# Eight PSUM banks dealt 3/3/2 in place of 2/4/2 among DFT pieces, first-layer and second-layer products

## The chip, the cores and the metric

The kernel runs on one core of one Trainium2 chip. The metric is device time in microseconds (us), the median of three runs; lower is better. Besides the runs, one execution was taken by the hardware profiler, and every view shown here comes from that one.

TensorE (PE) multiplies, ScalarE (ACT) and VectorE (DVE) work element by element, GpSimd (POOL) and SyncE (SP) mostly issue DMAs here. PSUM is the memory that matmuls write; it has eight banks, each 128 partitions by 512 fp32 values. Every PSUM tile of this kernel takes one bank.

## The reference

For each of 8 batches of 3008 tokens by 256 channels, a spectral filter along the tokens, and then a two-layer network with a periodic activation on all 24,064 tokens:

```python
X = np.fft.rfft(x, axis=1)
Y = X * (filt_r + 1j * filt_i)[None]
x = np.fft.irfft(Y, n=3008, axis=1).reshape(24064, 256)
h = x @ w_in                                  # 256 -> 2048
g = h + np.sin(alpha * h) ** 2 / (alpha + 1e-09)
out = g @ w_out                               # 2048 -> 256
```

## The kernel before, in words

**The network.** It is worked in 48 chunks of tokens, 12 for each pair of batches: 44 of 512 columns and 4 of 384 (those with `c0 == 2560`: chunks 5, 17, 29 and 41). For each chunk, `hidden(k, jb)` runs for jb = 0 to 15: two accumulating matmuls (L540, one for each half of the 256 channels) write a first-layer block of 128 features by 512 tokens into a PSUM tile `ph`; ACT takes its sine with a phase (L544, `cos_all<-ph`); DVE joins both into `v` (L545, `v<-cos_all,ph`). Because L545 reads `ph` a second time, the bank is free only when L545 has ended. `project(k, u)` makes the second layer: for each block of 128 tokens, 16 matmuls with 256 columns (L557, `po<-w,v`) in two halves of eight, then an ACT copy (L565) and DMAs to the output.

**The spectral filter.** A DFT of 3008 = 47 x 64 in two stages, forward and back, for each batch, as small pieces: `first` (tile `pa`, L181), `forward` (`pb`, L201, evicted by ACT at L204, then the two halves are swapped by DMA into `xs`), `product` and `cross` (DVE, L215, L221, L222), `inverse` (`pc`, L232) and `last` (`pd`, L254). Most evictions go through `evac` (L160 on ACT, L162 on DVE), two on ACT for each one on DVE. Batch 0 is worked ahead of the network with tiles of the same names (`pa` L399, `pb` L431, `pc` L453, `pd` L343); warming matmuls on idle data (L381) fill TensorE's early waits. `last` writes `y`, the network's input.

**The order.** The kernel is scheduled by hand; each engine runs its list in the order in which the program issues it. The main loop goes through 49 chunk places of eight half-steps j: two first-layer products of chunk k, then pieces that are due (`slot`), then that half-step's share of second-layer halves of chunk k-1, then pieces again. Which halves fall on half-step j is `range(n_half * j // 8, n_half * (j + 1) // 8)`, with n_half = 8 for a chunk of 512 columns and 6 for one of 384. Pieces have due times in half-steps (`put`); the last `pd` matmul starts at 729.9 us.

**The pools.** PSUM tiles come from three pools: `fps` for all spectral pieces (tag "f"), `hps` for first-layer products (`ph`), and, before the network starts, for some of batch 0's tiles (`pa` of two in three pieces, `pb`, one `pd`), for warming tiles and for alpha's spread; `ops` for `po` and a few early tiles. A tile's first matmul waits until the instructions that read the bank's earlier tile have ended. TensorE works strictly in order, so whatever stands behind a waiting matmul waits too.

Of the kernel before, what the change touches and what calls it, by code (L numbers as in the profile page):

```python
# [15 lines left out]
PSUM = bass.MemoryType.PSUM  # L16
# [46 lines left out]
def kernel(  # L63
# [28 lines left out]
    def pool(name, bufs, space=None):  # L92
        kw = {} if space is None else {"space": space}
        return ctx.enter_context(tc.tile_pool(name=name, bufs=bufs, **kw))
# [8 lines left out]
    opool = pool("op", 3)  # L103
    vpool = pool("vp", 2)
    dpool = pool("dram", 2, DRAM)
    fps = pool("fps", 2, PSUM)
    hps = pool("hps", 4, PSUM)
    ops = pool("ops", 2, PSUM)

    wf_t = cpool.tile([NR, NK], FP16)  # L110
# [46 lines left out]
    def evac(dst, src, on_act=None):  # L157
        flip[0] = (flip[0] + 1) % 3
        if flip[0] if on_act is None else on_act:
            marks["act"] = nc.scalar.copy(out=dst, in_=src)  # L160
        else:
            marks["dve"] = nc.vector.tensor_copy(out=dst, in_=src)  # L162
# [213 lines left out]
    def warm_pe(n):  # L376

        warmed.append(n)
        ps = hps.tile([128, 512], FP32, name=f"warm_{len(warmed)}", tag="h")
        for i in range(n):  # L380
            nc.tensor.matmul(out=ps, lhsT=idle[:, 0:128], rhs=idle[:, 0:512], start=True, stop=True)  # L381
# [7 lines left out]
    def cast_x0(h):  # L389

        cs = slice(4 * C * h, 4 * C * h + 4 * C)
        evac(x0[0].rearrange("p n c -> p (n c)")[:, cs], x32[0:NR, cs], False)
# [1 line left out]
    cast_x0(0)  # L394
    nc.vector.reciprocal(out=rec, in_=al)
    for i in range(16):
        own, tag = (fps, "f") if i % 3 == 2 else (hps, "h")
        ps = own.tile([128, 512], FP32, name=f"pa_0_{i}", tag=tag)
        nc.tensor.matmul(out=ps, lhsT=wf0_t[0:NR], rhs=x0[i // 4][:, 2 * (i % 4):2 * (i % 4) + 2, :],  # L399
                         start=True, stop=True)  # L400
        evac(t1_0[:, 2 * i:2 * i + 2], ps.rearrange("p (n k c) -> p n c k", n=2, k=2), i % 2)
        if i == 1:
            warm_pe(3)
            cast_x0(1)
        if i < 15 and i % 4 == 3:
            warm_pe((2, 2, 2, 1)[i // 4])
# [56 lines left out]
    for g in range(6):  # L463
        own, tag = (t2pool, "t2") if g < 3 else (gpool, "g")
# [225 lines left out]
```

## Time and profile before

| what | value |
|---|---|
| runs, median (lowest to highest) | 789.85 us (789.4 to 790.68) |
| profiled execution, span | 786.7 us |
| granted TensorE clock, mean | 1.000 |
| first matmul of the first product of the network (L540) | 36.8 us |
| L540, one matmul with 512 columns, median | 379 ns |
| L544 on 128x512, median | 597 ns |
| L545 on 128x512, median | 681 ns |
| evictions of pa: ACT / DVE, median | 582 / 679 ns |
| evictions of pc: ACT / DVE, median | 592 / 685 ns |
| evictions of pb (ACT), median | 586 ns |

The span is from the first to the last instruction of the profiled execution; the runs' times include what lies around it, 3.15 us at the median. A matmul's own duration is longer than its distance to the next one, since they are pipelined: two readings of TensorE's progress, the busy time and the distance of starts, have to be kept apart. In groups, the part behind the bar is busy time, the mean of one instruction, and the idle time of that engine just before such instructions with what ended it. In the timeline, a row is start, length from the first start to the last end, engine, line, operation, tiles and shapes, and how many instructions it merges.

Busy time by stretch, from the windows view (all engines in us):

| stretch, us | what runs | PE | DVE | ACT | clock |
|---|---|---|---|---|---|
| 0 to 37 | batch 0's filter, weights | 32.20 | 30.34 | 24.97 | 1.00 |
| 37 to 48 | chunk 0, no second layer yet | 10.28 | 9.69 | 10.51 | 1.00 |
| 48 to 73 | batch 0's last pieces, batch 1's first | 22.31 | 19.39 | 18.81 | 1.00 |
| 73 to 86 | batch 1, forward | 12.81 | 10.73 | 10.78 | 1.00 |
| 86 to 118 | batch 1, filter and inverse | 31.12 | 30.55 | 25.62 | 1.00 |
| 118 to 130 | | 11.97 | 9.71 | 9.78 | 1.00 |
| 130 to 787 | the regular part | 652.83 | 547.21 | 515.99 | 1.00 |

### The profile page before, as it was taken

How to read it: one execution, taken by the hardware profiler on the slowest of the kernel's cores; microseconds unless marked ns; L12 is line 12 of the kernel's file. 1: busy time of each engine (PE TensorE's matmuls, PEld its weight loads, DVE VectorE, ACT ScalarE, POOL GpSimd, SP SyncE). 2: the span in 40 equal slices, each digit the busy share in tenths (PEclk: the TensorE clock that was granted, in tenths of full speed). 3: DMA queues.
4: the chain of work that ended last, by engine and by line, in shares of the span. 5: the costliest groups of instructions: out<-in, count | busy, mean ns of one | idle time of the engine just before them, and what ended most of it. 6: DMA issues, size and time to landing. Idle time of an engine off the chain costs nothing.

```text
span 786.7 us, 16619 instructions
## 1 busy us (share of the span) xinstructions
PE 773.5 (98%) x5799; PEld 535.0 (68%) x5799; DVE 657.6 (84%) x1172; ACT 616.5 (78%) x1208; POOL 79.5 (10%) x125
## 2 busy tenths in 40 slices
PE   8998999999999999999999999999999999999998
PEld 4756766666667766777666766777666776766666
DVE  7887997899878997799977998799987999777773
ACT  5797878888878887888877888788887887777674
POOL 6442000200020000200020000200002000000000
PEclk9999999999999999999999999999999999999999
DMA  9965568665473646554575454845556243421111
GB/s 213 258 131 157 113 145 223 153 123 133 134 198 84 134 99 195 143 120 110 120 200 128 103 106 139 224 87 113 129 155 181 61 99 81 117 62 28 41 41 54
DMA packets 87692, 100.99 MB, mean 128 GB/s; under 512 B 14488, under 2 KB 75944, under 8 KB 87608
## 3 DMA queue, kind: packets, MB, share of 16 engines
q1 hardware_dynamic: 78032, 73.73, 34.5%
q0 software_dynamic: 9360, 26.15, 17.7%
q8 instruction: 45, 0.74, 0.4%
q14 instruction: 39, 0.32, 0.1%
q10 hardware_dynamic: 216, 0.05, 0.0%
HBM read 55.72 MB, written 46.66 MB: 130 GB/s over the span
## 4 chain that ended last, share of the span: by engine, by line
PE 89%; DVE 5%; ACT 2%; DMA 2%; issue 1%; SPq 1%; ACTq 0%; DVEq 0%
PE po L557 39%; PE ph L540 38%; PE pa L181 3%; PE pd L254 2%; DVE v L545 2%; PE pb L201 2%; PE pc L232 2%; DMA xs<-xf 1%; ACT cos_all L544 1%; DMA al<-in_moe_alpha_dram 1%; PE warm L381 1%; PE pc L453 0%; SPq L585 0%; ACT t_h L160 0%; DVE filt_t L162 0%
## 5 line engine op out<-in xcount | busy, mean ns | idle before, releaser
L545 DVE SCALAR_TENSOR_TENSOR v<-cos_all,ph 128x512 f16<-128x512 f32 (+1 forms) x768 | 483.0, 672 | 108.1 <-ACT cos_all L544 104.8
L544 ACT ACTIVATE cos_all<-ph 128x512 f32<-128x512 f32 (+1 forms) x768 | 411.1, 592 | 93.9 <-PE ph L540 92.9
L540 PE MATMUL ph<-y,w 128*128 128x512 f16 (+1 forms) x1536 | 388.4, 374 | 1.7 <-DVE y L162 0.9
L557 PE MATMUL po<-w,v 128*128 128x256 f16 x3008 | 389.5, 272 | 0.0
L557 PEld LDWEIGHTS <-v 128*128 128x128 f16 x3008 | 288.3, 98 | 77.7 <-issue 1.4
L540 PEld LDWEIGHTS <-w 128*128 128x128 f16 x1536 | 147.9, 98 | 106.5 <-issue 6.1
L565 ACT COPY o<-po 128x512 f32<-128x512 f32 (+1 forms) x97 | 55.6, 574 | 20.2 <-PE po L557 12.9
L204 ACT CAST xf<-pb 128x512 f16<-128x512 f32 x84 | 50.0, 595 | 16.4 <-PE pb L201 12.7
L193 POOL DMA_DIRECT2D t<-d x56 | 36.4, 669 | 204.6 <-DMA out_dram<-o 99.8
L160 ACT CAST t_h<-pa 96x512 f16<-96x512 f32 x74 | 43.3, 585 | 10.6 <-PE pa L181 10.5
L141 POOL DMA_DIRECT2D x<-in_x_dram x32 | 17.1, 536 | 298.2 <-PE pc L232 171.2
L160 ACT CAST y<-pd 128x376 f16<-128x376 f32 (+1 forms) x82 | 39.5, 482 | 8.8 <-PE pd L254 5.3
L254 PEld LDWEIGHTS <-t_a 96*128 96x128 f16 x448 | 31.3, 97 | 18.7 <-issue 0.4
L181 PE MATMUL pa<-x,wf_t 94*96 94x512 f16 x112 | 42.3, 381 | 1.6 <-ACT t_h L160 1.3
L160 ACT CAST g<-pc 128x512 f16<-128x512 f32 x58 | 34.4, 593 | 8.0 <-PE pc L232 7.7
L222 DVE TENSOR_TENSOR p<-p,xs 128x512 f16<-128x512 f16 x84 | 35.7, 425 | 2.9
L254 PE MATMUL pd<-wi_t,t_a 96*128 96x94 f16 x448 | 37.1, 204 | 0.0
L221 DVE TENSOR_TENSOR xs<-xs,filt_t 128x512 f16<-128x512 f16 x84 | 35.2, 420 | 0.8 <-DMA xs<-xf 0.8
L215 DVE TENSOR_TENSOR p<-xf,filt_t 128x512 f16<-128x512 f16 x84 | 35.2, 419 | 0.0
L232 PE MATMUL pc<-p,e_t 128*128 128x256 f16 x168 | 32.1, 273 | 0.8 <-ACT xf L204 0.5
L201 PE MATMUL pb<-t,d_t 128*128 128x256 f16 x168 | 32.1, 272 | 0.2
L162 DVE CAST y<-pd 128x376 f16<-128x376 f32 (+2 forms) x46 | 24.9, 544 | 1.5 <-PE pd L343 1.0
(66 smaller groups left out, 264.4 us busy)
## 6 DMA issues: line engine op xcount, KB each, us to landing
x<-in_x_dram POOLq DMA_DIRECT2D x30, 376.0 KB, 4.9
d<-t_h SPq DMA_DIRECT2D x28, 384.0 KB
t<-d POOLq DMA_DIRECT2D x56, 192.0 KB, 4.6
xs<-xf SPq DMA_DIRECT2D x168, 64.0 KB
d<-g SPq DMA_DIRECT2D x56, 192.0 KB
t_a<-d SPq DMA_DIRECT2D x28, 384.0 KB
out_dram<-o SPq DMA_DIRECT2D x104, 80.0 KB
w_out<-in_moe_w_out_dram SPq DMA_DIRECT2D x2, 1024.0 KB
```

Source lines behind the costliest of these rows:

```text
L160: marks["act"] = nc.scalar.copy(out=dst, in_=src)
L181: marks["pe"] = nc.tensor.matmul(out=ps[0:NK, :], lhsT=wf_t, rhs=self.x[ch][:, 2 * j:2 * j + 2, :], start=True, stop=True)
L193: nc.gpsimd.dma_start(out=self.t2[g][64 * p:64 * p + 64, :, :], in_=self.d1[a0:a0 + 6, :, :].rearrange("s n c -> n s c"))
L201: nc.tensor.matmul(out=ps[:, i, :], lhsT=d_t[:, s, :], rhs=self.t2[s // 6][:, s % 6, :], start=True, stop=True)
L204: nc.scalar.copy(out=self.xf[u], in_=ps)
L232: nc.tensor.matmul(out=ps[:, i, :], lhsT=e_t[:, 2 * w + i, :], rhs=pt[:, i, :], start=(k == 0), stop=(k == len(pr) - 1))
L254: nc.tensor.matmul(out=psv[:, i, :], rhs=wi_t, start=True, stop=True, lhsT=t4_h[ch // 2][0:NK, n0 % 16 + i, cb * 128:cb * 128 + 128])
L540: nc.tensor.matmul(out=ps[:, 0:n], lhsT=w1[:, cb, jb * 128:jb * 128 + 128], rhs=y_cols[:, cb, c0:c0 + n], start=(cb == 0), stop=(cb == 1))
L544: nc.scalar.activation(out=cs[:, 0:n], in_=ps[:, 0:n], func=AFT.Sin, bias=float(np.pi / 2))
L545: marks["snake"] = nc.vector.scalar_tensor_tensor(out=v[k][:, jb, 0:n], in0=cs[:, 0:n], scalar=-1.0, in1=ps[:, 0:n], op0=ALU.add, op1=ALU. ...
L557: nc.tensor.matmul(out=pso[k][:, t % 2, :], lhsT=v[k][:, jb, 128 * t:128 * t + 128], rhs=w2[:, jb, :], start=(jb == 0), stop=(jb == 15))
L565: nc.scalar.copy(out=o[:, i0:t % 2 + 1, :], in_=pso[k][:, i0:t % 2 + 1, :])
```

## The change

Two numbers of banks are exchanged, and the rule by which the 16 first-stage pieces of batch 0 take turns between the two pools changes with them: every second piece instead of every third goes to `fps`. `ops` keeps two. The sum stays at eight banks.

```diff
@@ -103,8 +103,8 @@
     dpool = pool("dram", 2, DRAM)
-    fps = pool("fps", 2, PSUM)
-    hps = pool("hps", 4, PSUM)
+    fps = pool("fps", 3, PSUM)
+    hps = pool("hps", 3, PSUM)
     ops = pool("ops", 2, PSUM)
@@ -394,7 +394,7 @@
     for i in range(16):
-        own, tag = (fps, "f") if i % 3 == 2 else (hps, "h")
+        own, tag = (fps, "f") if i % 2 else (hps, "h")
         ps = own.tile([128, 512], FP32, name=f"pa_0_{i}", tag=tag)
```

## The prediction

> **What bounds the kernel now.** I read the page first, for the busiest engine and the heaviest groups, then the durations of everything that touches a first-layer bank (ph), then the instructions in order of time at three places.
>
> ```profile
> span 786.7 us, 16619 instructions
> PE 773.5 (98%) x5799; PEld 535.0 (68%) x5799; DVE 657.6 (84%) x1172; ACT 616.5 (78%) x1208; POOL 79.5 (10%) x125
> ...
> PEclk9999999999999999999999999999999999999999
> ...
> PE 89%; DVE 5%; ACT 2%; DMA 2%; issue 1%; SPq 1%; ACTq 0%; DVEq 0%
> ...
> L545 DVE SCALAR_TENSOR_TENSOR v<-cos_all,ph 128x512 f16<-128x512 f32 (+1 forms) x768 | 483.0, 672 | 108.1 <-ACT cos_all L544 104.8
> L544 ACT ACTIVATE cos_all<-ph 128x512 f32<-128x512 f32 (+1 forms) x768 | 411.1, 592 | 93.9 <-PE ph L540 92.9
> L540 PE MATMUL ph<-y,w 128*128 128x512 f16 (+1 forms) x1536 | 388.4, 374 | 1.7 <-DVE y L162 0.9
> L557 PE MATMUL po<-w,v 128*128 128x256 f16 x3008 | 389.5, 272 | 0.0
> ```
>
> TensorE sets the end: 98% busy, 89% of the chain, full clock in all 40 slices, while DVE and ACT idle for want of it. Busy time overstates a pipelined engine, so I check with spacing: in the next fence eight matmuls with 512 columns take 1.89 us, so (1.89 - 0.38)/7 = 0.216 us from start to start. From 130 us to the end the starts follow each other at such intervals with only 1.4 us of waits in 650. So there a new wait on TensorE is paid in full, and a removed one is earned in full.
>
> ```profile
> 323.03 1.89 PE L540 MATMUL ph<-y,w 128*128 128x512 f16 x8
> ...
> 323.71 2.07 ACT L544 ACTIVATE cos_all<-ph 128x512 f32<-128x512 f32 x4
> ...
> 324.34 1.88 DVE L545 SCALAR_TENSOR_TENSOR v<-cos_all,ph 128x512 f16<-128x512 f32 x3 [0.94 <-ACT cos_all L544]
> ```
>
> This is the timeline at the start of chunk 18 (start, duration, engine). A ph bank is taken by the first of two matmuls (L540), read by the sine (L544) and read again by L545, which frees it. How long it is held: 0.216 to the second matmul, 0.414 from that start to the sine's start, 0.60 of sine, 0.03, 0.68 of L545, 0.053 until the next matmul can start (that last gap is the same wherever a matmul in this trace waited for DVE): 1.99 us if both engines come at once.
>
> **The change part by part.** The instructions and their order are the same on every engine; only which bank each tile gets, and so who waits, changes. No DMA or queue moves. There are three effects.
>
> *1. One bank less for first-layer products, from chunk 6 on (130 us to the end).* Product m will wait for L545 of product m-3 instead of m-4. So I take, for each of the 768, the trace's end of L545 of m-3 plus 0.053, minus the start of the first matmul of m: where it is positive, the product would be late. The worst place is structural. A chunk of 384 columns has six halves of second-layer work for eight half-steps, and the loop gives none to j = 0 and j = 4; there four first-layer products run without a second-layer one between them. In the fence the fourth starts at 323.03 + 6 x 0.216 = 324.32, but the first's L545 ends at 324.34 + 0.68 and frees the bank at 325.08: 0.76 late. This happens twice in each of chunks 6, 18, 30 and 42: 0.707, 0.704, 0.764, 0.762, 0.764, 0.760, 0.764, 0.707, together 5.93 us.
>
> The rest are 28 single products, 0.03 to 0.59 us late, where DVE does something else before L545, as here:
>
> ```profile
> 374.63 1.03 PE L540 MATMUL ph<-y,w 128*128 128x512 f16 x4
> ...
> 374.92 0.69 DVE L162 CAST g<-pc 128x512 f16<-128x512 f32 x1
> ...
> 376.30 0.42 DVE L222 TENSOR_TENSOR p<-p,xs 128x512 f16<-128x512 f16 x1
> 376.37 1.03 PE L540 MATMUL ph<-y,w 128*128 128x512 f16 x4
> ...
> 376.64 1.28 DVE L545 SCALAR_TENSOR_TENSOR v<-cos_all,ph 128x512 f16<-128x512 f32 x2
> ```
>
> The product begun at 374.63 has its L545 only at 376.64, behind an eviction and three filter products; the second product of the next step, due at 376.37 + 0.43 = 376.80, would wait until 377.38: 0.58. The 28 sum to 5.21. Four of them come a few us after another one with DVE busy in between, so that the first shift already covers them in part (4 x 0.20), and three of 0.05 follow a 0.76 and vanish (0.15): 4.3. Together 10.2 us, at most 11.1 if nothing is covered.
>
> *2. One bank more for DFT pieces, from 130 us on.* These waits now cost 1.44 us: 0.17 + 0.07 at pd, 0.24 + 0.18 at pb, 3 x 0.21 at pa, 2 x 0.08 at pc. One of them:
>
> ```profile
> 197.68 1.03 PE L540 MATMUL ph<-y,w 128*128 128x512 f16 x4
> 198.03 0.68 DVE L162 CAST t_h<-pa 96x512 f16<-96x512 f32 x1
> ...
> 198.76 0.38 PE L181 MATMUL pa<-x,wf_t 94*96 94x512 f16 x1
> ```
>
> pa is due at 197.68 + 4 x 0.216 = 198.55, and starts 0.05 after the eviction's end at 198.71: 0.21 lost. With three banks it takes one that was freed earlier. All nine go. Net from 130 us: 10.2 - 1.4 = +8.8.
>
> *3. Before 130 us.* Here lateness is not additive, because DVE or ACT is the limit for stretches, so I carry each start forward with the trace's durations.
> - 37 to 48 us: chunk 0 has no second-layer work at all. L540 already waits 2.6 us there, at DVE's pace of 0.60 per product (0.68 less 0.08 overlap). With three banks the pace is 1.99/3 = 0.665, so 15 x 0.07 = 1.0 more, 0.7 at the fourth product (its bank's first L545 starts only at 38.12), and 0.7 for the y evictions on ACT and DVE that fall into the ring: +2.4.
> - 48 to 86 us: bank waits of pieces stand at 3.1 us (pa 0.12, 0.28, 0.83, 0.83; pd 0.51, 0.29; pb 0.23). Carried forward 0.6 remain, and the wait at 68.7 us for y, which DVE's own queue sets, grows by 0.5: -2.0, so +0.4 since 37 us.
> - 86 to 118 us: DVE is 95% busy and ACT waits up to 1.7 us for swapped halves (xs<-xf). The late products, carried, cost 3.9 if the swaps shift with the kernel and 2.6 if they land when they land now; waits of 2.1 and 1.9 us go away: +0.7 to +1.8.
> - Before 37 us: pb_0 and warming tiles share three banks, pc_0 has three. Its chain runs through ACT and DVE, and at most 0.65 us of pc waits can go (28.9 to 30.2 us); at the forward pieces (18 to 21 us) about as much can come. I take 0, +-0.5.
>
> Sum before 130 us: +1.1 to +2.2, taken as +1.7. Whole: 8.8 + 1.7 = +10.5 us. The span goes from 786.7 to 797.2; the runs' median is 789.85, 3.15 above the profiled span, which I keep: **800.3 us**, 1.3% slower.
>
> Bounds: below, if half the single products fall away and nothing is lost before 130 us: 5.9 + 2.2 - 1.4 = +6.7, 796.5. Above, if none is covered (11.1), no piece's wait goes, and 2.2 + 0.5 before: +13.8, 803.7.
>
> One rule speaks for a much worse end: the Trainium skill, "TensorE: Matmul & The Clock Gate", section "A second HAM failure mode: psum-queue depth-cycling", says that short idles between matmul groups which cycle through PSUM banks can make the clock gate fall and rise again. In this trace fifteen such waits in a row from 38.9 to 47.2 us (0.08 to 0.7 us each) leave the granted clock at 1.00. By the page's figures (half rate for a window of some 3.4 us) 35 waits would cost an estimated 35 x 1.7 = 60 us; by the row, nothing. I go by the row.
>
> **The rivals.**
> - *Faster: only the pieces feel banks.* Their waits from 37 us on, pa 2.7, pd 1.3, pb 0.65, pc about 1.5, are 6.1 us; if ph were free after the sine, 1.26 us after its first matmul, no fourth product would come before its bank (3 x 0.43 = 1.29). Then 789.85 - 6.1 = 783.7. It decides from the point where L545 takes no PSUM input; but its row reads "cos_all,ph". 2%.
> - *Even: half and half.* Only the eight places cost (5.9), the pieces earn 6.1: 789.7. For it: page and waits show DVE idle 16%. Against: the single late products are where DVE is busy with filter work, and half the earning lies before 73 us, where y and DVE hold the start anyway. 3%.
> - *Much slower: every late product pays in full.* All 72 sum to 35.6 us; less 6 earned: 819. Against: 9.9 of them are one shift counted 15 times in chunk 0, 14.0 lie between 86 and 118 us, mostly likewise. 3%.
>
> **How the numbers follow.** Forecast 92%, rivals as given. Range 797.0 to 803.5: the bounds, a little inside. A measurement of this kernel can tell about 0.2% (1.6 us) from no change; slower 95%, same 3%, faster 2%.
>
> **What would show it.** PE waits of L540 for DVE's L545 grow from 0.6 to several us, with 0.7 to 0.8 us holes at the fourth and twelfth product of chunks 6, 18, 30 and 42, and holes near 0.4 to 0.6 at the places like 376.8; PE waits for evictions of pa, pb, pc and pd vanish after 130 us; PE busy share falls by one point; DVE and ACT durations stay. It is wrong if L540's holes are missing, or if pieces wait as before.

## The result, and the profile after

The changed kernel takes 799.89 us (median of 4 runs, 798.94 to 800.23) against 790.02 us of the kernel before on the same chip: ratio 1.013, 95% interval 1.0116 to 1.0145. The medians are 9.9 us apart; the profiled spans, 786.7 and 797.1 us, 10.4. The forecast was 800.3 us and a span of 797.2.

The page of the changed kernel, its span, busy times and the four groups that were shown before:

```profile
span 797.1 us, 16616 instructions
...
PE 776.2 (97%) x5799; PEld 534.9 (67%) x5799; DVE 659.7 (83%) x1172; ACT 620.4 (78%) x1208; POOL 79.9 (10%) x125
...
L545 DVE SCALAR_TENSOR_TENSOR v<-cos_all,ph 128x512 f16<-128x512 f32 (+1 forms) x768 | 484.8, 672 | 117.8 <-ACT cos_all L544 112.9
L544 ACT ACTIVATE cos_all<-ph 128x512 f32<-128x512 f32 (+1 forms) x768 | 414.5, 591 | 102.2 <-PE ph L540 100.4
L540 PE MATMUL ph<-y,w 128*128 128x512 f16 (+1 forms) x1536 | 394.1, 374 | 12.3 <-DVE v L545 10.2
L557 PE MATMUL po<-w,v 128*128 128x256 f16 x3008 | 389.4, 272 | 0.0
```

None of the four groups became slower: their means are those of before to 1 ns. What moved is one idle time. L540's went from 1.7 to 12.3 us, 10.2 of it for L545. The waits view of TensorE says the same, and shows that the pieces wait for no eviction any more in the regular part (who waited <- for what: us in total, times, longest):

```profile
PE ph L540 <- DVE v L545: 10.2, 21, 0.7
...
PE ph L540 <- DVE y L162: 1.4, 1, 1.4
...
PE pb L201 <- DMA t<-d: 0.7, 1, 0.7
```

These totals hide some of the loss. A matmul of 512 columns shows 0.379 us, but the next may start 0.216 us after it; so up to 0.163 us of each wait lies under the matmul before it and is not idle time on the page. After 130 us the waits view has 5.4 us in 11 waits for L545, while the distances of starts give 10.5 us. So the account below is made from starts: TensorE's order is the same in both kernels, and each matmul's start after, less its start before, is the shift so far.

| stretch of before, us | forecast, us | measured, us |
|---|---|---|
| 0 to 37 | 0, +-0.5 | -1.0 |
| 37 to 48 | +2.4 | +2.7 |
| 48 to 86 | -2.0 | -1.15 |
| 86 to 130 | +0.7 to +1.8 | +0.9 |
| 130 to the end | +8.8 | +9.0 |
| sum | +10.5 | +10.4 |

The start of chunk 18 in the changed kernel, in order of time:

```profile
326.31 1.24 PE L540 MATMUL ph<-y,w 128*128 128x512 f16 x5
...
327.41 2.69 DVE L545 SCALAR_TENSOR_TENSOR v<-cos_all,ph 128x512 f16<-128x512 f32 x4 [0.95 <-ACT cos_all L544]
328.15 0.59 PE L540 MATMUL ph<-y,w 128*128 128x512 f16 x2 [0.60 <-DVE v L545]
```

The first row begins at the second of the matmuls, so the fourth product (the seventh matmul) was due at 326.31 + 5 x 0.216 = 327.39. The first L545 ends at 327.41 + 0.68 = 328.09, and the matmul starts 0.06 later: a hole of 0.76 us (0.60 of it visible as idle). The eight holes of this kind measure 0.706, 0.707, 0.763, 0.763, 0.763, 0.762, 0.763 and 0.706, together 5.93 us.

And a piece of the first DFT stage, the one that had waited 0.21 us at 198.76 before:

```profile
200.55 1.03 PE L540 MATMUL ph<-y,w 128*128 128x512 f16 x4
200.89 0.68 DVE L162 CAST t_h<-pa 96x512 f16<-96x512 f32 x1
...
201.41 0.38 PE L181 MATMUL pa<-x,wf_t 94*96 94x512 f16 x1
```

Due at 200.55 + 4 x 0.216 = 201.41, it starts at 201.41, before the eviction on DVE has ended (201.57): its bank is another one.

### The profile page after: what moved, and what is told of

It is laid out like the page before. It is cut to its first block, busy times and chain, and to the rows that moved or that the text cites. A ratio compares the mean times of both kernels' runs of the same rounds, so it can differ in the third digit from the quotient of the medians.

```text
span 797.1 us, 16616 instructions
## 1 busy us (share of the span) xinstructions
PE 776.2 (97%) x5799; PEld 534.9 (67%) x5799; DVE 659.7 (83%) x1172; ACT 620.4 (78%) x1208; POOL 79.9 (10%) x125
## 4 chain that ended last, share of the span: by engine, by line
PE 85%; DVE 6%; DMA 3%; ACT 3%; issue 2%; SPq 0%; POOL 0%; ACTq 0%; DVEq 0%; POOLq 0%
PE po L557 38%; PE ph L540 36%; PE pa L181 3%; DVE v L545 3%; PE pd L254 2%; PE pb L201 2%; PE pc L232 2%; ACT cos_all L544 2%; DMA xs<-xf 1%; DVE t_a L413 1%; DMA t<-d 1%; DMA cos_all<-in_x_dram 1%; PE pb L431 1%; DVE xs L221 0%; DVE p L222 0%
## 5 line engine op out<-in xcount | busy, mean ns | idle before, releaser
L545 DVE SCALAR_TENSOR_TENSOR v<-cos_all,ph 128x512 f16<-128x512 f32 (+1 forms) x768 | 484.8, 672 | 117.8 <-ACT cos_all L544 112.9
L540 PE MATMUL ph<-y,w 128*128 128x512 f16 (+1 forms) x1536 | 394.1, 374 | 12.3 <-DVE v L545 10.2
L540 PEld LDWEIGHTS <-w 128*128 128x128 f16 x1536 | 147.8, 98 | 120.6 <-issue 25.1
L215 DVE TENSOR_TENSOR p<-xf,filt_t 128x512 f16<-128x512 f16 x84 | 35.1, 418 | 0.0
```

Source lines behind the costliest of these rows:

```text
L540: nc.tensor.matmul(out=ps[:, 0:n], lhsT=w1[:, cb, jb * 128:jb * 128 + 128], rhs=y_cols[:, cb, c0:c0 + n], start=(cb == 0), stop=(cb == 1))
L545: marks["snake"] = nc.vector.scalar_tensor_tensor(out=v[k][:, jb, 0:n], in0=cs[:, 0:n], scalar=-1.0, in1=ps[:, 0:n], op0=ALU.add, op1=ALU. ...
```

## The experiments

The ratios are to runs of the kernel before on the same chip, 13 runs each: median 788.84 us for the pools 2/3/2, 3/4/1 and the pool of six and for the first kernel with the bank freed by the sine, 788.52 us for the others. TensorE runs the same matmuls in the same order in all of these kernels, so starts can be compared as above.

**One bank less for the first layer, and nothing for the pieces.**

```diff
-    hps = pool("hps", 4, PSUM)
+    hps = pool("hps", 3, PSUM)
```

> Pools 2/3/2 (pieces, first layer, second layer): the first layer loses its fourth bank, the pieces get nothing, one bank lies idle. Theory (every late product waits for L545, and the pieces' third bank gave part of it back): the late products carried forward cost 14.5 us, so 804.5 us (802 to 807), and the wait of L540 for L545 is as in the changed kernel. Rival (only the eight places after the 384-column chunks cost): 790 + 5.9 = 796. Rival (the new turn of banks among the early pieces or anything else in the pieces' pool is what costs): 790.

Measured: 802.52 us, ratio 1.0173 (1.0156 to 1.019). TensorE's waits in this kernel:

```profile
PE ph L540 <- DVE v L545: 9.9, 20, 0.7
...
PE pa L181 <- ACT t_h L160: 1.3, 2, 0.7
```

The wait for L545 is that of the changed kernel, and the pieces' waits of before are back. By starts it is 13.6 us behind the kernel before, of which 10.1 come after 130 us. So the loss of the fourth bank is worth more than the whole change, and the third bank of the pieces gave part of it back. The forecast (802 to 807) holds, near its lower end; both rivals (796, 790) are out.

**The changed kernel, with the bank freed by the sine.**

```diff
-            out=v[k][:, jb, 0:n], in0=cs[:, 0:n], scalar=-1.0, in1=ps[:, 0:n],
+            out=v[k][:, jb, 0:n], in0=cs[:, 0:n], scalar=-1.0, in1=cs[:, 0:n],
```

> The changed kernel (3/3/2) with L545 taking the cosine tile for both of its inputs, so that h itself is left out of v: a first-layer bank is then held by the sine alone, 1.26 us instead of 1.99. Theory (the wait is for L545's second read): three products take 3 x 0.43 = 1.29 us, no fourth comes too early, L540's waits for DVE vanish and the pieces keep their third bank: 3.9 us less than before by the starts carried forward and 1.0 from the stretch before 37 us, so 785 us (783 to 787). Rival (a bank more or less costs by itself, through the order or the sharing of PSUM): stays at 797 to 800.

Measured: 795.66 us, ratio 1.0083 (1.0058 to 1.0108): neither number. By starts, the stretch from 130 us on is 1.2 us shorter than before, as the theory has it, but the stretch from 37 to 48 us is 6.9 us longer. The groups by form from 38 to 48 us of this kernel:

```profile
L545 DVE SCALAR_TENSOR_TENSOR v<-cos_all 128x512 f16<-128x512 f32 x6 | 11.0, 1902 | 1.1 <-ACT cos_all L544 1.1
L514 POOL TENSOR_TENSOR w<-w_out,rec_t 128x1024 f16<-128x1024 f32 x3 | 5.7, 1908 | 0.0
```

and the same two groups in that stretch of the kernel before:

```profile
L545 DVE SCALAR_TENSOR_TENSOR v<-cos_all,ph 128x512 f16<-128x512 f32 x16 | 9.8, 683 | 1.3 <-ACT cos_all L544 1.3
...
L514 POOL TENSOR_TENSOR w<-w_out,rec_t 128x1024 f16<-128x1024 f32 x3 | 5.7, 1908 | 0.0
```

The edit took PSUM out of L545's inputs (both now lie in SBUF, the memory of the kernel's other on-chip tiles), and L545 became 1.90 us long on average in place of 0.68 while GpSimd scaled the weights: 2.49 to 2.54 us for the three that ran beside one of the three L514, 0.68 again for the one behind them. GpSimd's own time stayed at 1.908. So the experiment had changed two things in that stretch. The Trainium skill has the reason, in "SBUF — State Buffer", section "Who interferes with whom": a VectorE instruction with two inputs in SBUF contends with a GpSimd instruction that reads SBUF, while one with at most one SBUF input does not (certain faster modes aside). The two pairs of rows agree with both halves of it.

A third thing came after it. TensorE now waited up to 1.8 us at a time in chunk 0, and its granted clock fell to half for 6.8 us, where the kernel before has 1.00. In this view a row is a stretch, its length, the busy time (and number) of PE, PEld, DVE, ACT and POOL, the granted clock, and the DMA engines' share and GB/s:

```profile
41.58:44.99 3.41, 1.06 (x6) 0.50 (x5) 3.41 (x2) 0.77 (x2) 3.40 (x4) 1.00 0.88 136
45.00:51.80 6.80, 4.16 (x10) 1.39 (x10) 6.80 (x9) 4.38 (x9) 2.83 (x3) 0.50 0.92 155
```

In the profiled execution this cost little, at most 0.9 of the 6.9 us: by starts 6.1 of them come at waits for sines that the long L545 held up. The mean granted clock was 0.991 to 0.996 in the four runs, against 0.999 or 1.000 in the kernel before, and the profiled one had the 0.996; so the median holds more of this than the profile shows, and how much is open.

**The same, from chunk 3 on only.**

```diff
-            out=v[k][:, jb, 0:n], in0=cs[:, 0:n], scalar=-1.0, in1=ps[:, 0:n],
+            out=v[k][:, jb, 0:n], in0=cs[:, 0:n], scalar=-1.0, in1=(cs if k > 2 else ps)[:, 0:n],
```

> As the run before with L545 taking the cosine tile twice, but only from chunk 3 on (72 us and later; there h is left out of v); chunks 0 to 2 are as in the changed kernel. That keeps L545 with two inputs from the stretch up to 50 us, where GpSimd scales the weights. Theory: until 72 us as the changed kernel, after 130 us no wait of L540 for DVE at all and no wait of pieces, so that stretch is 1.4 us shorter than before in place of 9.0 longer: 10.4 us less than the changed kernel and about 1 less between 86 and 118 us, 788.5 us (787 to 790.5), span near 785.5. Rival (three banks cost by themselves): 797 to 800.

Measured: 789.82 us, ratio 1.0016 (1.0002 to 1.0031), where the changed kernel stands at 1.013. L545 and L540 by form from 130 to 750 us:

```profile
L545 DVE SCALAR_TENSOR_TENSOR v<-cos_all 128x512 f16<-128x512 f32 x591 | 380.3, 686 | 73.6 <-ACT cos_all L544 70.8
...
L540 PE MATMUL ph<-y,w 128*128 128x512 f16 x1184 | 302.8, 379 | 0.0
```

L545 is as long as ever (686 ns), and L540 waits for nothing. From 130 us on this kernel gains 1.2 us on the kernel before, with the same three banks for the first layer with which the changed kernel loses 9.0. So a bank less costs nothing by itself; what costs is that L545 holds it. The time lies in the forecast's range, and the rival (797 to 800) is out. Around 128 us the profiled execution waited 3.1 us for a DMA (`pd` for `t_a<-d`), which was not expected and is more than the 1.3 us by which the median misses 788.5. That load was issued at 126.3 us, and at 120.5 us in the kernel before; why so late is open.

**A third bank for the pieces with four for the first layer, and one without.** Pools 3/4/1 and 2/4/1 (pieces, first layer, second layer); 2/4/1 has the second of these two edits alone.

```diff
-    fps = pool("fps", 2, PSUM)
+    fps = pool("fps", 3, PSUM)
...
-    ops = pool("ops", 2, PSUM)
+    ops = pool("ops", 1, PSUM)
```

> Pools 3/4/1: the pieces get their third bank from the second layer, the first layer keeps four. Theory: the pieces' waits (4.9 us carried forward after 37 us) and 1.0 us before 37 us go; the second layer's single bank waits for its copy (L565), 3.5 us carried forward: 788.3 us (786.5 to 790.5). Rival (the third bank of the pieces is worth nothing, the whole +10 was one-sided): 790 + 3.5 = 793.5.

> Pools 2/4/1: before with one bank taken from the second layer and given to nobody; against 3/4/1 it shows the worth of the pieces' third bank while the first layer keeps four. Theory: after 37 us the pieces' third bank is worth 4.9 us less what DMAs and DVE take back, some 3 us as the run of 3/4/1 shows in its starts; this one is then 792.5 us (791 to 794). Rival (the third bank is worth nothing to the pieces): the same as 3/4/1, 789.4.

Measured: 789.41 us (1.0007, 0.9996 to 1.0017) with three, 792.95 us (1.0056, 1.0039 to 1.0072) with two. Both lie in their ranges, and both rivals are out. The difference, 0.0049 of 788.6 us = 3.9 us, give or take 1.5 by the two intervals, is the worth of the pieces' third bank. In the kernel 3/4/1 the price shows at the second layer:

```profile
L557 PE MATMUL po<-w,v 128*128 128x256 f16 x3008 | 389.9, 272 | 2.1 <-ACT o L565 2.0
```

With one bank a second-layer tile waits for the copy of the one before. By starts, most of it (2.3 us) falls in the last chunk, where no first-layer work stands between two tiles; up to there the kernel with 3/4/1 is 3.0 us ahead of before. The 1.0 us expected before 37 us did not come: its first network product starts at 37.2 us, for 36.8 before, and from 16.7 to 20.1 us its granted clock was 0.50.

**The old turn of banks among batch 0's first pieces.**

```diff
-        own, tag = (fps, "f") if i % 2 else (hps, "h")
+        own, tag = (fps, "f") if i % 3 == 2 else (hps, "h")
```

> The changed kernel with the old turn of banks among batch 0's 16 first pieces (every third to the pieces' pool): tells which part of the change made the first 37 us 1.0 us shorter. Theory (the shorter start is the third bank of the pieces, at the forward and inverse pieces of batch 0, not the turn): the same within 0.5 us, 799.5 (798.5 to 801). Rival (the turn does it): 1.0 us more, 800.9, and the first product of the network starts at 37.0 us in place of 36.0.

Measured: 799.53 us, 1.0132 (1.0117 to 1.0147): the same as the changed kernel. Its first network product starts at 36.3 us, where the changed kernel's starts at 35.8 and that of before at 36.8, so one profile each would give the turn 0.5 of the 1.0 us. But the two kernels with the bank freed by the sine have the pools and the turn of the changed kernel up to there, and theirs starts at 36.2 us in both. So profiles of the same start differ by 0.4 us, and nothing here gives the turn any part; the rival (800.9 us, 37.0 us) is not seen.

**Two banks for the first layer.** Pools 4/2/2.

```diff
-    fps = pool("fps", 3, PSUM)
-    hps = pool("hps", 3, PSUM)
+    fps = pool("fps", 4, PSUM)
+    hps = pool("hps", 2, PSUM)
```

> Pools 4/2/2: the first layer loses one bank more. Theory (a product waits for L545 of the one two earlier, held 1.99 us): starts carried forward give 84 us more than before, 874 us (862 to 886), with the wait at nearly every half-step. Rival (the wait of 3/3/2 comes from the turn or the order, not from how long a bank is held): 800 to 820.

Measured: 873.85 us in one run, beside 788.52. TensorE near 400 us, in order of time:

```profile
400.55 1.04 PE L557 MATMUL po<-w,v 128*128 128x256 f16 x8
...
400.62 1.28 DVE L545 SCALAR_TENSOR_TENSOR v<-cos_all,ph 128x512 f16<-128x512 f32 x2 [0.72 <-ACT cos_all L544]
...
401.43 0.38 PE L232 MATMUL pc<-p,e_t 128*128 128x256 f16 x2
...
401.65 1.03 PE L540 MATMUL ph<-y,w 128*128 128x512 f16 x4
...
402.73 1.04 PE L557 MATMUL po<-w,v 128*128 128x256 f16 x8
...
402.96 1.28 DVE L545 SCALAR_TENSOR_TENSOR v<-cos_all,ph 128x512 f16<-128x512 f32 x2 [0.27 <-ACT cos_all L544]
...
403.70 0.59 PE L540 MATMUL ph<-y,w 128*128 128x512 f16 x2
```

At 401.65 the pair of products starts without waiting: the L545 for its bank had ended at 400.62 + 0.68 = 401.30, and a piece stood in between besides. At 403.70 only the eight second-layer matmuls stand in between: they were streamed by 402.73 + 8 x 0.109 = 403.60, the L545 of the last pair's first product ended at 402.96 + 0.68 = 403.64, and the next pair starts 0.06 later. With three banks a half-step without second-layer work or with a late DVE was needed for a hole; with two, any plain half-step is at the edge. So the 85 us are many small holes: after 130 us some 400 products start late, half of them by less than 0.17 us, together 76 us. The size came out as forecast (84 us) with the same hold, the same order and one bank less; the rival (800 to 820) is out.

**One pool of six for pieces and first layer.** The two pools become one, so that a bank goes to whichever tile comes next; the other tiles of `hps` go there with the old turn, and the order of the instructions is the same.

```diff
-    fps = pool("fps", 2, PSUM)
-    hps = pool("hps", 4, PSUM)
+    fps = pool("fps", 6, PSUM)
+    hps = fps
...
-        ps = hps.tile([128, 512], FP32, name=f"ph_{k}_{jb}", tag="h")
+        ps = hps.tile([128, 512], FP32, name=f"ph_{k}_{jb}", tag="f")
```

> One pool of six banks for pieces and first-layer products together, two for the second layer: a bank goes to whichever tile comes next. Theory: where no pieces run, first-layer products have six banks, where they do, four or so, and a piece hardly waits; carried forward 4.3 us less than before after 37 us, and up to 1.0 before: 785 us (783 to 788), faster than both kernels. Rival (pieces push first-layer products back to three banks' distance, so it is no better than the changed kernel): 797 to 800.

Measured: 784.98 us (783.38 to 786.71), ratio 0.9951 (0.9932 to 0.9969), faster than both kernels. The waits of TensorE:

```profile
PE ph L540 <- DVE y L162: 1.6, 1, 1.6
...
PE pd L254 <- DMA t_a<-d: 1.4, 1, 1.4
PE ph L540 <- ACT xf L204: 0.9, 1, 0.9
...
PE ph L540 <- DVE v L545: 0.6, 2, 0.4
PE ph L540 <- ACT t_h L160: 0.4, 1, 0.4
```

Waits for L545 are as few as with four banks, and waits of `pa` for its evictions are gone as with three. The pool of six has a price of its own: twice a first-layer product waited for a piece's eviction (`xf`, `t_h`), both before 103 us; from 130 to 750 us L540 has no idle time before it. The rival (797 to 800) is out. The profiled execution took 786.71 us: by starts it was 3.1 us ahead of before at 86 us and lost 1.9 until 130 us, 1.4 of it to a load (`t_a<-d`) that lands after TensorE now gets there; that load is what a next step would have to look at.

## Why the prediction was right, step by step

- *The eight places after the 384-column chunks*: forecast 5.93 us, measured 5.93. Each is a hold of 2.00 to 2.06 us less the 6 x 0.216 = 1.30 us that three products take, and the change touches neither.
- *The single late products*: forecast 4.3, measured 4.5 by starts. The subtraction for those that an earlier shift covers was needed: uncovered they are 5.2.
- *The pieces' waits after 130 us*: all nine (1.44 us) went. Net from 130 us: 9.0 for 8.8. That L545's second read is the cause was then an argument from the order of events; the kernel that frees the bank after the sine from chunk 3 on shows it, and the one with nothing given to the pieces shows the sign of each part.
- *37 to 48 us*: forecast +2.4, measured +2.7. The pace of the ring, 1.99 us for three products, is there where no eviction of `y` comes between: L545 starts at 37.11 and 39.11 us, at 43.15 and 45.14. So is the 0.7 us at the fourth product. What makes up the 0.3 us more is not shown.
- *48 to 86 us*: forecast -2.0, measured -1.15. The pieces' gains and the longer wait for `y` (1.57 for 1.06) came as forecast. What the step lacked is a wait of 0.83 us at the first `pb` of batch 1 (0.7 as idle time) for its load `t<-d`. TensorE was ready 0.26 us later than before, but the load, issued 0.38 us later, took 5.2 us to land in place of 3.6; why is open. The forecast named no wait for a load there: its sentence that no DMA moves holds for the program's order, not for the times.
- *86 to 130 us*: measured +0.9, inside the two ends.
- *0 to 37 us*: forecast 0 +- 0.5, measured -1.0, outside, and not by the banks. Of the 1.0 us, 0.75 is there by the third first-stage piece of batch 0 (8.46 us before, 7.71 after), and up to there TensorE waits for casts of the input, which stand behind loads on VectorE. The first cast in the kernel before, and in the changed one:

```profile
5.49 0.69 DVE L162 CAST x<-cos_all 94x1024 f16<-94x1024 f32 x1 [2.18 <-DMA cos_all<-in_x_dram]
```

```profile
4.91 0.76 DVE L162 CAST x<-cos_all 94x1024 f16<-94x1024 f32 x1 [1.60 <-DMA cos_all<-in_x_dram]
```

  From there to 37 us the gain is 0.25 us, inside the step's range. That an early load of 0.75 us and the missed wait for a load of 0.83 us nearly cancel is luck.
- *From span to time*: the 3.15 us added to the span are not what lies around it, as the text on the time before has it. In every run that lists both, the time is 1.7 to 1.9 us above its own span; the rest is that the profiled execution of before was some 1.3 us shorter than the median. In the changed kernel the same difference happened to be 2.8 us, which makes most of the 0.4 us between forecast and measurement. That it was so near is luck too.
- *The clock*: it stayed at 1.00 in the changed kernel with some 60 waits of this kind, and at 1.00 in the kernel with two banks, with some 400 late starts. The rule that the forecast cites, on short idles, shows in none of these. The clock did fall in the first kernel with the bank freed by the sine, to 0.50 after waits at banks of 1.0 and 1.8 us and within a third of 1.8, when TensorE had been busy for 1.06 of 3.41 us. So going by the row was right for the waits that this change makes (up to 0.85 us), and is not shown for longer ones in close order.
- *The rivals*: "faster" fell by the sign; "even" by the single late products (4.5 us of the 10.5); "much slower" because a shift, once paid, covers the later products of its stretch: chunk 0, where that rival counts 9.9 us, lost 2.7. (The forecast's own rule for late products gives 71 of them and 35.1 us in the trace of before, where it has 72 and 35.6.)

## What to carry to other kernels

Before taking a PSUM bank away, measure how long one tile holds its bank, from its first matmul to the end of its last reader, and compare that with how soon the producer comes round to it, place by place and in the tightest place first: here 1.99 us against the 1.29 us after which the fourth product in a row starts. If the tight engine does nothing but stream, each such hole is paid in full, and starts, not idle times, show its size. Where two kinds of tiles need their banks at different times, one pool for both can serve better than a split: here 2/4 and 3/3 both lose to a shared six.

## What was not expected of the hardware

L545 with both inputs in SBUF took 2.49 to 2.54 us beside GpSimd's elementwise instructions, 1.90 on average in that stretch, and 0.68 with one input in PSUM; GpSimd's 1.908 us did not change. After 130 us, where GpSimd issues only DMAs, L545 with two SBUF inputs takes 0.686. An edit that only moves an operand from PSUM to SBUF can so cost a factor of 3.7 in one stretch and nothing in the next. Nor was it expected that TensorE's granted clock would fall to 0.50 in that kernel, after 3.41 us in which TensorE was busy for 1.06; that its waits are the cause is inferred from the order in time.
